# Transposes of a fused attention and GLU kernel: from the tensor engine to the DMA queues

## The chip, the cores and the metric

The kernel runs on one core of a Trainium2 chip. A core has a tensor engine (PE, with its weight loads shown as PEld), a vector engine (DVE), a scalar engine (ACT), GpSimd (POOL), and SyncE (SP), which here only issues DMAs. Matmul results land in PSUM; the other operands live in SBUF. The metric is the device time of one execution in microseconds (us). Before the change it was 374.96 us (median of 15 runs, 373.54 to 377.10). Each run carries a state, fast or slow; fast runs alone are compared here.

## The reference, cut to what matters

The input is 2048 tokens of width 640, in bfloat16. After a layernorm, the tokens go through a 32-head attention with a recurrent memory over four segments of 512 tokens, and through a gated unit. The two results are multiplied and added to the input.

```python
xn = layernorm(x)                               # no affine part
for s in range(4):                              # segments of 512 tokens
    a_dot = softmax(q @ k.T * scale + mask) @ v
    a_mem = phi(q) @ M / (phi(q) @ z + 1e-6)    # memory of earlier segments
    o     = g * a_mem + (1 - g) * a_dot
    M    += phi(k).T @ v;   z += sum(phi(k))    # phi(t) = t+1 if t>0 else exp(t)
s = o @ wo
h = sigmoid(xn @ w_gate) * (xn @ w_up);   y = h @ w_down
out = x + s * silu(y)
```

## The kernel before

The program is scheduled by hand. A segment has 24 slots, one for each of 8 head groups times 3 units of keys. A slot issues scores, one large Exp on ACT and the product with V. Between these, `fill` feeds dense matmuls (gate, up, down) to PE at an even pace, and a plan hangs smaller pieces on slots: the next segment's layernorm and projections, the memory read (`mem_part`, slots 0 to 7) and the memory update (slots 9 and 10). The plan fixes the order of each engine's instructions. Most matmul results share three PSUM buffers (`ps_d`, tag "d"), so PE waits when a buffer it wants has not been read out yet (two such waits are shown below).

Three tensors are needed in the other orientation. Each is transposed on PE, 128 tokens at a time, in a group of five 128x128 transposes into one PSUM buffer, followed by a copy:

```python
ps_d = ctx.enter_context(tc.tile_pool(name="ps_d", bufs=3, space=PSUM))

def ln_transpose(n, j, xn, eng):                 # normalized x
    pT = ps_d.tile([P, DC, P], BF, name="pT", tag="d")
    for c in range(DC):                          # DC = 5
        nc.tensor.transpose(pT[:, c, :], xn[:, c * P:(c + 1) * P], ident[:])
    ... nc.vector.tensor_copy(xnT_of[n][:, :, j * P:(j + 1) * P], pT[:])

def phiK_tok(n, j):                              # phi(K), to tokens on partitions
    pk = ps_d.tile([P, DC, P], BF, name="pk", tag="d")
    for c in range(DC):
        nc.tensor.transpose(pk[:, c, :], seg[n]["kt"][:, c, j * P:(j + 1) * P], ident[:])
    ... nc.vector.tensor_copy(t[:], pk[:].rearrange("p c t -> p (c t)"))

def out_T(n, j):                                 # attention output, before @ wo
    po = ps_d.tile([P, DC, P], BF, name="po", tag="d")
    for c in range(DC):
        nc.tensor.transpose(po[:, c, :], s["odot"][:, j, c * P:(c + 1) * P], ident[:])
    ... nc.scalar.mul(oT[:], po[:], 0.25)
```

K and Q also make a round trip through DRAM (`Kd`, `Qd`) to be laid out by head; this is there before and after.

## Time and profile before

| what | value | view |
|---|---|---|
| span of the profiled execution | 373.7 us | page |
| PE busy | 351.8 us, 94% | page, busy table |
| DVE and ACT busy | 231.9 us each, 62% | page, busy table |
| chain of work that ended last | 74% PE | page, chain |
| one group of five transposes | 0.29 us of PE | timeline |

The page of the kernel before, its span and busy table, the DMA totals, and the chain by engine (lines left out between them):

```profile
span 373.7 us, 8613 instructions
PE 351.8 (94%) x3569; PEld 196.9 (53%) x3569; DVE 231.9 (62%) x523; ACT 231.9 (62%) x246; POOL 103.4 (28%) x172
...
DMA packets 21527, 25.60 MB, mean 69 GB/s; under 512 B 1648, under 2 KB 20208, under 8 KB 21488
...
PE 74%; ACT 10%; DVE 8%; issue 3%; DMA 2%; POOL 1%; SPq 0%; POOLq 0%; ACTq 0%
```

PE is the engine to relieve. A busy PE is not PE at its peak, so the worth of a transpose is read from the timeline. This is the timeline of PE (start, length, line, operation, tiles, shapes, count):

```profile
45.90 0.41 PE L464 MATMUL Sps<-QT,KT 21*128 21x384 bf16 x8
46.24 0.45 PE L299 MATMUL pk<-ident,ktd 128*128 128x128 bf16 x5
46.53 1.24 PE L346 MATMUL gp<-xnT,Wg 128*128 128x512 bf16 x5
```

The group is printed as 0.45 us long, but the next group starts 0.29 us after it. That step is what a group costs. The copies out of PSUM are read from the groups of instructions (busy us, mean ns, then idle time before them):

```profile
L387 ACT ACTIVATE oT<-po 128x640 bf16<-128x640 bf16 x12 | 8.4, 700 | 1.2 <-PE po L385 0.9
...
L203 DVE COPY xnT<-pT 128x640 bf16<-128x640 bf16 x12 | 5.8, 484 | 1.1 <-PE pT L198 1.1
L301 DVE COPY phiktok<-pk 128x640 bf16<-128x640 bf16 x12 | 5.8, 482 | 0.0
```

PE is not full everywhere. In stretches of 10 us (us, then for each engine its busy time and count, then granted clock, DMA share, GB/s) it drops where a segment starts, while DVE is nearly full:

```profile
core 0: us, PE busy (x) PEld busy (x) DVE busy (x) ACT busy (x) POOL busy (x), PEclk, DMA share, GB/s
120.00:130.00 10.00, 8.45 (x100) 4.88 (x99) 9.62 (x28) 6.96 (x7) 2.37 (x4) 1.00 0.01 2
200.00:210.00 10.00, 8.50 (x94) 4.47 (x95) 9.69 (x26) 6.56 (x8) 3.27 (x4) 1.00 0.01 2
210.00:220.00 10.00, 8.39 (x90) 4.97 (x89) 8.29 (x25) 4.56 (x5) 3.32 (x6) 0.83 0.05 18
```

Among the waits of PE (us in total, times, longest) are two in which `gp` (a gate product) stands still for results that it does not use; what it waits for, by the code, is one of the three PSUM buffers:

```profile
PE gp L346 <- ACT oT L387: 1.0, 1, 1.0
...
PE gp L346 <- DVE aa L401: 0.9, 1, 0.9
```

### The profile page before, as it was taken

What the parts mean: (1) busy time and instruction counts of PE and PEld (TensorE: products, weight loads), DVE (VectorE), ACT (ScalarE), POOL (GpSimd) and SP (SyncE); (2) the same over time, 40 slices, a digit from 0 to 9 for tenths busy, and PEclk for the clock granted to TensorE, in tenths of its full rate; (3) what the DMA queues carried; (4) which work ended last, traced back from release to release, by engine and by line L of the source; (5) the groups of instructions that cost most, each with busy time, mean ns of one, the idle gap of its engine ahead of it and who ended that gap; (6) DMA issues with size and microseconds to landing.
All of it is one profiled execution on the core that took longest, in us unless ns stands there. A gap on an engine that the chain in (4) does not pass through costs nothing.

```text
span 373.7 us, 8613 instructions
## 1 busy us (share of the span) xinstructions
PE 351.8 (94%) x3569; PEld 196.9 (53%) x3569; DVE 231.9 (62%) x523; ACT 231.9 (62%) x246; POOL 103.4 (28%) x172
## 2 busy tenths in 40 slices
PE   6999999999999899999998799999989999999992
PEld 2643456555645466455565356555436755545661
DVE  5465966456549997756548977746744575533354
ACT  2436766656868765665777656555776677666730
POOL 7600232222232222222223222222212222221314
PEclk9999999999999999999999899999999999999997
DMA  7976820012521010012520001011402000100001
GB/s 237 381 260 197 251 88 3 0 44 69 136 67 46 3 35 19 19 44 92 153 68 6 0 19 37 19 44 47 125 3 71 3 2 19 38 18 3 2 2 70
DMA packets 21527, 25.60 MB, mean 69 GB/s; under 512 B 1648, under 2 KB 20208, under 8 KB 21488
## 3 DMA queue, kind: packets, MB, share of 16 engines
q1 hardware_dynamic: 20176, 21.12, 18.6%
q10 hardware_dynamic: 1312, 3.93, 2.7%
q8 instruction: 28, 0.46, 0.5%
q14 instruction: 11, 0.09, 0.1%
HBM read 17.05 MB, written 7.86 MB: 67 GB/s over the span
## 4 chain that ended last, share of the span: by engine, by line
PE 74%; ACT 10%; DVE 8%; issue 3%; DMA 2%; POOL 1%; SPq 0%; POOLq 0%; ACTq 0%
PE yp L369 13%; PE up L355 12%; PE gp L346 12%; PE psq L215 10%; PE Aps L488 7%; PE Sps L464 6%; ACT pt L472 6%; PE psv L273 5%; PE sp L399 4%; ACT mn L288 2%; DMA Wv<-in_A_wv_dram 2%; PE cps L259 1%; PE dm L312 1%; DVE omem L339 1%; DVE hT L358 1%
## 5 line engine op out<-in xcount | busy, mean ns | idle before, releaser
L472 ACT ACTIVATE pt<-Sps 128x2048 bf16<-128x2048 f32 (+1 forms) x96 | 152.9, 1593 | 41.3 <-PE Sps L464 39.9
L474 POOL TENSOR_SCALAR_AFFINE_SELECT pt<-pt 128x512 bf16<-128x512 bf16 x128 | 82.5, 655 | 254.7 <-ACT pt L472 254.7
L346 PE MATMUL gp<-xnT,Wg 128*128 128x512 bf16 x240 | 60.9, 385 | 3.2 <-DVE omem L339 1.1
L355 PE MATMUL up<-xnT,Wu 128*128 128x512 bf16 x240 | 59.7, 379 | 2.0 <-ACT tg L349 2.0
L369 PE MATMUL yp<-Wd,hT 128*128 128x320 bf16 x384 | 57.5, 299 | 0.0
L358 DVE SCALAR_TENSOR_TENSOR hT<-tg,up 128x512 bf16<-128x512 bf16 x48 | 32.6, 680 | 38.2 <-PE up L355 33.6
L488 PEld LDWEIGHTS <-pt 128*128 128x128 bf16 x1280 | 45.0, 96 | 20.1 <-issue 5.0
L488 PE MATMUL Aps<-V,pt 128*128 128x21 bf16 x1280 | 47.2, 173 | 2.6 <-DVE rm L336 1.0
L349 ACT ACTIVATE tg<-gp 128x512 bf16<-128x512 f32 x48 | 28.4, 596 | 24.7 <-PE gp L346 24.5
L369 PEld LDWEIGHTS <-hT 128*128 128x128 bf16 x384 | 35.2, 97 | 15.1 <-issue 2.2
L373 DVE SCALAR_TENSOR_TENSOR aa<-t,yp 128x320 bf16<-128x320 bf16 x32 | 15.5, 485 | 39.7 <-ACT t L372 39.7
L464 PE MATMUL Sps<-QT,KT 21*128 21x128 bf16 (+3 forms) x512 | 34.9, 302 | 0.6 <-ACT pt L472 0.4
L346 PEld LDWEIGHTS <-Wg 128*128 128x128 bf16 x240 | 21.0, 98 | 27.2 <-issue 6.5
L355 PEld LDWEIGHTS <-Wu 128*128 128x128 bf16 x240 | 21.2, 97 | 23.9 <-issue 3.9
L278 ACT CAST V<-psv 128x320 bf16<-128x320 f32 x32 | 13.7, 428 | 24.2 <-PE psv L273 24.0
L464 PEld LDWEIGHTS <-KT 21*128 21x128 bf16 x512 | 11.3, 91 | 30.8 <-issue 30.4
L273 PE MATMUL psv<-Wv,xnT 128*128 128x320 bf16 x160 | 26.1, 299 | 0.5 <-DMA Wv<-in_A_wv_dram 0.5
L372 ACT ACTIVATE t<-yp 128x320 bf16<-128x320 f32 x32 | 13.9, 436 | 19.5 <-PE yp L369 19.5
L215 PE MATMUL psq<-xnT,Wq 128*128 128x512 bf16 x100 | 24.3, 378 | 0.0
L215 PE MATMUL psq<-xnT,Wk 128*128 128x512 bf16 x100 | 24.3, 378 | 0.0
L220 DVE CAST ktd<-psq 128x512 bf16<-128x512 f32 x20 | 13.7, 687 | 15.8 <-PE psq L215 15.8
L399 PE MATMUL sp<-Wo,oT 128*128 128x320 bf16 x120 | 20.3, 300 | 1.0 <-DVE omem L339 1.0
(91 smaller groups left out, 363.7 us busy)
## 6 DMA issues: line engine op xcount, KB each, us to landing
KT<-Kd SPq DMA_DIRECT2D x32, 80.0 KB
QT<-Qd SPq DMA_DIRECT2D x32, 80.0 KB
out_dram<-xt SPq DMA_DIRECT2D x16, 160.0 KB
Wg<-in_B_w_gate_dram ACTq DMA_DIRECT2D x1, 1920.0 KB
Wu<-in_B_w_up_dram ACTq DMA_DIRECT2D x1, 1920.0 KB
xt<-in_A_x_dram SPq DMA_DIRECT2D x3, 640.0 KB
Wd<-in_B_w_down_dram SPq DMA_DIRECT2D x1, 1920.0 KB
Kd<-ktd SPq DMA_DIRECT2D x4, 384.0 KB
```

The source lines that it names most:

```text
L215: nc.tensor.matmul(ps[:], lhsT=W[:, k, c * P:(c + 1) * P], rhs=xnT_of[n][:, k, :], start=(k == 0), stop=(k == DC - 1))
L273: nc.tensor.matmul(ps[:], lhsT=xnT_of[n][:, k, j * P:(j + 1) * P], rhs=Wv[:, k, half * HD:(half + 1) * HD], start=(k == 0), stop=(k == DC ...
L346: nc.tensor.matmul(gp[:], lhsT=Wg[:, k, f * P:(f + 1) * P], rhs=xnT_of[n][:, k, :], start=(k == 0), stop=(k == DC - 1))
L349: nc.scalar.activation(tg[:], gp[:], ACT.Tanh, scale=0.5)
L355: nc.tensor.matmul(up[:], lhsT=Wu[:, k, f * P:(f + 1) * P], rhs=xnT_of[n][:, k, :], start=(k == 0), stop=(k == DC - 1))
L358: nc.vector.scalar_tensor_tensor(out=h[:], in0=seg[n]["tg"][:], scalar=1.0, in1=up[:], op0=ALU.add, op1=ALU.mult)
L369: nc.tensor.matmul(yp[:], lhsT=s["hT"][f][:, j * P:(j + 1) * P], rhs=Wd[:, f, hs], start=(f == 0), stop=(f == FC - 1))
L399: nc.tensor.matmul(sp[:], lhsT=s["po"][j][:, c, :], rhs=Wo[:, c, hs], start=(c == 0), stop=(c == DC - 1))
L464: nc.tensor.matmul(Sps[:, r, c0:c0 + ncol], lhsT=KT[32 * r:32 * r + E1, g, kb * P:(kb + 1) * P], rhs=QT[32 * r:32 * r + E1, g, q0:L], star ...
L472: nc.scalar.activation(pt[:, :, 0:ntot], Sps[:, :, 0:ntot], ACT.Exp, scale=SCALE)
L474: nc.gpsimd.affine_select(out=pt[:, :, c0:c0 + P], in_=pt[:, :, c0:c0 + P], compare_op=ALU.is_ge, fill=0.0, base=0, pattern=[[0, 4], [1, P ...
L488: nc.tensor.matmul(Aps[:, qb, r, :], lhsT=pt[:, r, off:off + P], rhs=V[n % 2][:, kb, 4 * g + r, :], start=(ui == 0 and r == 0 and qb == 0) ...
```

## The change

The intent is to take 180 of the transposes off PE. Each tensor is stored to DRAM in its natural layout (K is there already) and fetched with one 640 KB DMA transpose. The projection by `wo` starts four slots after the last store, to give the DMA time. phi(K) now acts on the transposed copy, and its Exp comes one slot after its minimum. In segment 0 it starts at slot 4, because its copy lands late. The factor 0.25 moves into the gates. SBUF room is found by letting `warm` share a buffer and by one `aa` buffer less. In segment 0, empty plan entries at slots 4 to 7 still count the time of four groups of transposes, so that `fill` puts less dense work there. Segment 0's layernorm and the last segment's output keep their PE transposes, because nothing could hide the latency there.

```diff
+    def ln_spill(n, j, xn):
+        nc.sync.dma_start(Xd[n % 2][j * P:(j + 1) * P, :], xn[:])
+
+    def ln_dmaT(n):
+        xnT_of[n] = xpool.tile([P, DC, L], BF, name="xnT")
+        nc.sync.dma_start_transpose(out=xnT_of[n][:], in_=Xd[n % 2][:])
...
-    def phiK_tok(n, j):
-        pk = ps_d.tile([P, DC, P], BF, name="pk", tag="d")
...
+    def k_tok(n):
+        seg[n]["ktok"] = stg.tile([P, 4, D], BF, name="ktok")
+        nc.sync.dma_start_transpose(out=seg[n]["ktok"][:], in_=Kd[n % 2][:])
...
-    def out_T(n, j):
-        po = ps_d.tile([P, DC, P], BF, name="po", tag="d")
...
+        nc.sync.dma_start(Od[n % 2][j * P:(j + 1) * P, :], s["odot"][:, j, :])
+
+    def out_T(n):
+        oT = fpool.tile([P, DC, L], BF, name="oT", bufs=1)
+        nc.sync.dma_start_transpose(out=oT[:], in_=Od[n % 2][:])
...
         for part in range(2):
-            at(2 * part, 0, phi, n, "kt", "phik", part)
-            at(2 * part + 1, 0, phi_end, n, "phik", part)
+            s0 = 4 if n == 0 else 0
+            at(s0 + 2 * part, 0, phi_min, n, "ktok", "phik", 2 * part, 2 * part + 2)
+            at(s0 + 2 * part + 1, 0, phi_exp, n, "phik", 2 * part)
+            at(s0 + 2 * part + 2, 0, phi_end, n, "phik", 2 * part)
         for j in range(4):
-            at(1 + j, 0, stats, j)
-            at(5 + j, 0, norm, j)
-            at(4 + j, TR_NS, phiK_tok, n, j)
-            at(6 + j, TR_NS, lambda j=j: ln_transpose(m, j, st[j], nc.vector))
+            at(j, 0, stats, j)
+            at(4 + j, 0, norm, j)
+        at(7, 0, ln_dmaT, m)
...
-        return deque([[A(0)], [A(1), T(0)], [M(0, 0)], [A(2), T(1), M(0, 1)], [M(1, 0)], [A(3), T(2), M(1, 1)],
-                      [M(2, 0)], [T(3), M(2, 1)], [M(3, 0)], [M(3, 1)]])
+        return deque([[A(0)], [A(1)], [A(2)], [A(3), T], [], [], []] + [[M(j, h)] for j in range(4) for h in range(2)])
```

More of the change, by code (lines that the diff above doesn't have):

```diff
@@ L89 @@
     Kd = [dpool.tile([D, L], BF, name=f"Kd{i}") for i in range(2)]
+    Xd = [dpool.tile([L, D], BF, name=f"Xd{i}") for i in range(2)]
+    Od = [dpool.tile([L, D], BF, name=f"Od{i}") for i in range(2)]
     ctx.enter_context(tc.manual_schedule(
@@ L115 @@
     Wu = cpool.tile([P, DC, F], BF, name="Wu")
-    warm = cpool.tile([P, L], BF, name="warm")
-    nc.vector.memset(warm[:], 0.0)
+    warm = stg.tile([P, 3 * L], BF, name="mn")
+    nc.vector.memset(warm[:, 0:L], 0.0)
     load_x(0, split=4)
@@ L167, in gates @@
         gcol = cpool.tile([P, H], F32, name="gcol")
-        nc.vector.tensor_scalar(gcol[:], th[:], 0.5, 0.5, op0=ALU.mult, op1=ALU.add)
-        nc.vector.tensor_scalar(omg[:], th[:], -0.5, 0.5, op0=ALU.mult, op1=ALU.add)
+        nc.vector.tensor_scalar(gcol[:], th[:], 0.125, 0.125, op0=ALU.mult, op1=ALU.add)
+        nc.vector.tensor_scalar(omg[:], th[:], -0.125, 0.125, op0=ALU.mult, op1=ALU.add)
         nc.vector.reciprocal(ginv[:], gcol[:])
@@ L280, in do_V, with phi, phi_min, phi_exp @@
             nc.vector.tensor_copy(dst, src)
-    def phi(n, key, name, part):
-        c0, c1 = ((0, 3), (3, 5))[part]
+    def phi(n, key, name, c0, c1):
         s = seg[n]
         src = s[key][:, c0:c1, :]
-        mn = stg.tile([P, 3, L], BF, name="mn")
-        nc.vector.tensor_scalar(mn[:, 0:c1 - c0, :], src, 0.0, None, op0=ALU.min)
-        nc.scalar.activation(mn[:, 0:c1 - c0, :], mn[:, 0:c1 - c0, :], ACT.Exp)
-        nc.vector.tensor_scalar(src, src, 0.0, None, op0=ALU.max)
-        s[name, part] = (src, mn[:, 0:c1 - c0, :])
-    def phi_end(n, name, part):
-        dst, ex = seg[n][name, part]
-        nc.vector.tensor_tensor(dst, dst, ex, op=ALU.add)
-    def phiK_tok(n, j):
-        pk = ps_d.tile([P, DC, P], BF, name="pk", tag="d")
-        for c in range(DC):
-            nc.tensor.transpose(pk[:, c, :], seg[n]["kt"][:, c, j * P:(j + 1) * P], ident[:])
-        t = stg.tile([P, D], BF, name="phiktok", bufs=4)
-        nc.vector.tensor_copy(t[:], pk[:].rearrange("p c t -> p (c t)"))
-        seg[n]["ktok", j] = t
+        mn = stg.tile([P, 3 * L], BF, name="mn")
+        w = src.shape[1] * src.shape[2]
+        m = mn[:, 0:w].rearrange("p (c n) -> p c n", n=src.shape[2])
+        nc.vector.tensor_scalar(m, src, 0.0, None, op0=ALU.min)
+        nc.scalar.activation(m, m, ACT.Exp)
+        nc.vector.tensor_scalar(src, src, 0.0, None, op0=ALU.max)
+        s[name, c0] = (src, m)
+    def phi_min(n, key, name, c0, c1):
+        s = seg[n]
+        src = s[key][:, c0:c1, :]
+        mn = stg.tile([P, 3 * L], BF, name="mn")
+        w = src.shape[1] * src.shape[2]
+        m = mn[:, 0:w].rearrange("p (c n) -> p c n", n=src.shape[2])
+        nc.vector.tensor_scalar(m, src, 0.0, None, op0=ALU.min)
+        nc.vector.tensor_scalar(src, src, 0.0, None, op0=ALU.max)
+        s[name, c0] = (src, m)
+    def phi_exp(n, name, c0):
+        m = seg[n][name, c0][1]
+        nc.scalar.activation(m, m, ACT.Exp)
+    def phi_end(n, name, c0):
+        dst, ex = seg[n][name, c0]
+        nc.vector.tensor_tensor(dst, dst, ex, op=ALU.add)
+    def k_tok(n):
+        seg[n]["ktok"] = stg.tile([P, 4, D], BF, name="ktok")
+        nc.sync.dma_start_transpose(out=seg[n]["ktok"][:], in_=Kd[n % 2][:])
     def m_update(n, part):
@@ L312, in m_update @@
                 nc.tensor.matmul(dm[:, MOFF[c] - o0:MOFF[c + 1] - o0],
-                                 lhsT=seg[n]["ktok", j][:, c * P:(c + 1) * P],
+                                 lhsT=seg[n]["ktok"][:, j, c * P:(c + 1) * P],
                                  rhs=V[n % 2][:, j, h0:h1 + 1, :].rearrange("p h e -> p (h e)"),
@@ L364, in do_down @@
         if half == 0:
-            s["aa"][j] = fpool.tile([P, D], BF, name="aa", bufs=5)
+            s["aa"][j] = fpool.tile([P, D], BF, name="aa", bufs=4)
         hs = slice(half * HD, (half + 1) * HD)
@@ L379, in out_add @@
             nc.vector.tensor_tensor(s["odot"][:, j, :], s["odot"][:, j, :], s["omem"][:, j, :], op=ALU.add)
-    def out_T(n, j):
-        s = seg[n]
-        po = ps_d.tile([P, DC, P], BF, name="po", tag="d")
-        for c in range(DC):
-            nc.tensor.transpose(po[:, c, :], s["odot"][:, j, c * P:(c + 1) * P], ident[:])
-        oT = fpool.tile([P, DC, P], BF, name="oT")
-        nc.scalar.mul(oT[:], po[:], 0.25)
-        s["po"][j] = oT
+        nc.sync.dma_start(Od[n % 2][j * P:(j + 1) * P, :], s["odot"][:, j, :])
+    def out_T(n):
+        oT = fpool.tile([P, DC, L], BF, name="oT", bufs=1)
+        nc.sync.dma_start_transpose(out=oT[:], in_=Od[n % 2][:])
+        seg[n]["oT"] = oT
     def out_store(n, j):
@@ L398, in out_mm @@
         for c in range(DC):
-            nc.tensor.matmul(sp[:], lhsT=s["po"][j][:, c, :], rhs=Wo[:, c, hs],
+            nc.tensor.matmul(sp[:], lhsT=s["oT"][:, c, j * P:(j + 1) * P], rhs=Wo[:, c, hs],
                              start=(c == 0), stop=(c == DC - 1))
@@ L422, in tail_T @@
         if j % 2:
-            nc.vector.tensor_scalar(oT, po[:], 0.25, None, op0=ALU.mult)
+            nc.vector.tensor_copy(oT, po[:])
         else:
-            nc.scalar.mul(oT, po[:], 0.25)
+            nc.scalar.copy(oT, po[:])
     def tail_acc(i):
@@ L443, in tail_end @@
             nc.tensor.transpose(po[:, j, :], s["odot"][:, j, C4:D], ident[:])
-        oT = fpool.tile([P, DC, P], BF, name="oT")
-        nc.scalar.mul(oT[:, 0:4, :], po[:], 0.25)
+        oT = fpool.tile([P, DC, L], BF, name="oT", bufs=1)[:, 0, :].rearrange("p (j t) -> p j t", t=P)
+        nc.scalar.copy(oT, po[:])
         for i in range(8):
@@ L507, in keep_warm @@
         for _ in range(k):
-            nc.tensor.matmul(wps[:], lhsT=warm[:, 0:P], rhs=warm[:], start=True, stop=True)
+            nc.tensor.matmul(wps[:], lhsT=warm[:, 0:P], rhs=warm[:, 0:L], start=True, stop=True)
     keep_warm(11)
@@ L560 @@
     gates()
+    k_tok(0)
     nc.sync.dma_start(Wd[:], B_w_down.rearrange("(f p) n -> p f n", p=P))
@@ L591, in norm @@
         def norm(j):
-            st[j] = ln_norm(m, j, st["mv"], st["rs"])
+            ln_spill(m, j, ln_norm(m, j, st["mv"], st["rs"]))
         for part in range(2):
-            at(2 * part, 0, phi, n, "kt", "phik", part)
-            at(2 * part + 1, 0, phi_end, n, "phik", part)
+            s0 = 4 if n == 0 else 0
+            at(s0 + 2 * part, 0, phi_min, n, "ktok", "phik", 2 * part, 2 * part + 2)
+            at(s0 + 2 * part + 1, 0, phi_exp, n, "phik", 2 * part)
+            at(s0 + 2 * part + 2, 0, phi_end, n, "phik", 2 * part)
         for j in range(4):
-            at(1 + j, 0, stats, j)
-            at(5 + j, 0, norm, j)
-            at(4 + j, TR_NS, phiK_tok, n, j)
-            at(6 + j, TR_NS, lambda j=j: ln_transpose(m, j, st[j], nc.vector))
+            at(j, 0, stats, j)
+            at(4 + j, 0, norm, j)
+        at(7, 0, ln_dmaT, m)
+        for j in range(4 if n == 0 else 0):
+            at(4 + j, TR_NS, lambda: None)
         at(9, 800, m_update, n, 0)
@@ L617, in segment_plan @@
         at(18, 0, bound_dma, m, 0, [nc.sync])
-        at(18, 0, phi, m, "qt", "phiq", 0)
+        at(18, 0, phi, m, "qt", "phiq", 0, 3)
         at(19, 0, phi_end, m, "phiq", 0)
@@ L622, in segment_plan @@
         at(21, C_NS, bound_mm, m, 1, None)
-        at(21, 0, phi, m, "qt", "phiq", 1)
-        at(22, 0, phi_end, m, "phiq", 1)
+        at(21, 0, phi, m, "qt", "phiq", 3, 5)
+        at(22, 0, phi_end, m, "phiq", 3)
+        if m < NSEG - 1:
+            at(21, 0, k_tok, m)
         if n + 2 < NSEG:
@@ L630, in out_steps @@
         A = lambda j: (0, lambda: out_add(n, j))
-        T = lambda j: (TR_NS, lambda: out_T(n, j))
+        T = (0, lambda: out_T(n))
         M = lambda j, h: (V_NS, lambda: out_mm(n, j, h))
-        return deque([[A(0)], [A(1), T(0)], [M(0, 0)], [A(2), T(1), M(0, 1)], [M(1, 0)], [A(3), T(2), M(1, 1)],
-                      [M(2, 0)], [T(3), M(2, 1)], [M(3, 0)], [M(3, 1)]])
+        return deque([[A(0)], [A(1)], [A(2)], [A(3), T], [], [], []] + [[M(j, h)] for j in range(4) for h in range(2)])
     dense = deque()
```

## The prediction

> **What bounds the kernel.** The profile's busy table gives PE 351.8 of 373.7 us (94%), DVE and ACT 62% each; the chain of work that ended last is 74% PE. The stretches of 10 us show PE at 10.00 nearly everywhere; it falls to 8.4-9.1 only at the start (0-10), the tail (360-370), and where a new segment begins (120-140, 200-230), where DVE is at 8.1-9.7. There the waits list 2.6 us (118-145) and 4.7 us (200-232) of PE waiting, mostly for DVE (omem, aa, hT, rm) or ACT's oT. The clock drops to 0.83 in 210-220.
>
> **What the change removes.** For segments 1-3 the layernorm transposes (pT), for 0-2 those of phi(K) (pk) and of the attention output (po): 36 groups of five, 180 matmuls. In the timeline each group advances PE by 0.29 us (46.24 to 46.53): 36 x 0.29 = 10.4 us. Also DVE 24 x 0.48 = 11.6 us, ACT's oT 12 x 0.70 = 8.4 us, and 36 turns of the PSUM buffers.
>
> **What it adds.** 24 stores (12 xn, 12 odot tiles) of 160 KB and nine 640 KB DMA transposes on SP's queue. phi(K) acts on the transposed copy, same elements, its Exp one slot later. The 0.25 moves into the gates, free.
>
> **Is the DMA latency hidden?** Queues are nearly idle after 50 us (mean 69 GB/s). The plain 640 KB x load at 112-115 us takes about 3 us, near 250 GB/s. The Trainium skill, "DMA: Bandwidth & Descriptors", section "Latency and other measured facts", gives about 261 GB/s for DMA transposes; its page "VectorE: DVE Perf Modes", section "The three transpose paths", gives 1309 ns for one 128x128 block, which, if blocks did not overlap, would be 20 x 1.3 = 26 us for ours. No trace here shows which. My estimate: 4-8 us from issue to landing, plus about 2.5 us for the store. A slot is about 3.45 us (83 us / 24). xnT has about 3.5 slots (12 us) from the last norm to its first use, oT about 4 slots (14 us), ktok 3 slots before phi(K) and far more before its matmuls. SP issues in order, so a late odot store delays xn stores and xnT behind it; I expect under 1 us of PE wait per segment from it.
>
> **Sum.** 376.6 - 10.4 (PE) - 2.5 (less waiting at segment starts, as DVE loses 3.9 us per segment and ACT 2.8) + 1.3 (new exposure to xnT/oT) = **365.0 us**, range 359 to 374. Faster by over 2% (under 369.1): 0.75; within 2%: 0.17; slower by over 2%: 0.08.
>
> **What would show each step.** Right: PE has 180 matmuls less and its busy time falls by about 10 us; ACT about 8, DVE about 12 less; no PE wait over 1 us released by the xnT or oT transposes; PE nearer 10 in 120-140 and 200-230.
>
> **What would make it wrong.** (1) Transposes slow (over 10 us): PE would wait on the xnT DMA before the first K projection of segments 1-3, on oT before sp, and DVE on ktok; at 26 us that costs some 15 us per segment and the change is slower. (2) The transpose holding up SP's queue, so that KT/QT relayouts or Wd land late. (3) Segment starts bound by ACT's Exp or by DVE work that stays (mem_part, hT): then PE work saved there is returned as waiting and the gain shrinks to 5-7 us, within 2%.

## More of the kernel before

The granted clock was 0.50 from 212.1 to 215.5 us, from the second of two short gaps of PE on (in brackets: idle time before, and what ended it):

```profile
210.95 0.44 PE L299 MATMUL pk<-ident,ktd 128*128 128x128 bf16 x5 [0.75 <-DVE hT L358]
212.25 2.29 PE L346 MATMUL gp<-xnT,Wg 128*128 128x512 bf16 x5 [0.86 <-DVE aa L401]
```

A group of `gp` usually takes 1.24 us. From group start to group start in that stretch (2.09 us for `gp`, where 1.08 is usual, and less for the three groups after it), I estimate that the half clock cost this execution 1.4 us. Not every execution has it: of the 25 fast runs of this kernel in the calls of the experiments, seven have a mean clock of 0.990 or less and average 376.2 us, and the other 18, at 0.993 or more, average 374.3.

## The result, and the profile after

The changed kernel took 361.05 us (median of 12 runs, 359.69 to 366.03; the last was a slow run), against 374.96 us before. The ratio is 0.9628, with a 95% interval of 0.9601 to 0.9656: faster, by about 13.9 us. Ratios here are the mean time of one kernel's fast runs over that of the other's of the same rounds, so they are not quite the ratio of the medians.

The page of the changed kernel, same parts as above:

```profile
span 358.4 us, 8274 instructions
PE 341.6 (95%) x3389; PEld 185.9 (52%) x3389; DVE 221.0 (62%) x499; ACT 223.8 (62%) x234; POOL 104.5 (29%) x172
...
DMA packets 48309, 35.40 MB, mean 99 GB/s; under 512 B 25360, under 2 KB 46992, under 8 KB 48272
...
PE 75%; ACT 9%; DVE 9%; POOL 2%; issue 2%; DMA 2%; SPq 0%; POOLq 0%; ACTq 0%
```

PE has 180 matmuls and 10.2 us of busy time less, DVE 10.9 us and ACT 8.1 us less. PE's idle time, span less busy, went from 21.9 to 16.8 us. PE is still the bound. Part of this is luck: the execution profiled before lost about 1.4 us to the half clock, mostly as PE busy time, and this one has no half clock before its tail. The 23,712 added packets under 512 B are nearly all the nine transposes: 640 KB in packets of 256 B is 2560 packets each.

The stretches where segments start (the second segment's first Exp is now at 109 us, the third's at 189; before, at 112 and 195):

```profile
110.00:120.00 10.00, 9.35 (x95) 4.34 (x93) 9.59 (x26) 7.16 (x8) 3.07 (x4) 1.00 0.24 69
120.00:130.00 10.00, 9.46 (x96) 4.43 (x95) 8.90 (x24) 6.83 (x8) 4.37 (x6) 1.00 0.10 35
190.00:200.00 10.00, 9.36 (x102) 5.25 (x101) 9.59 (x27) 7.39 (x9) 2.72 (x4) 1.00 0.06 20
200.00:210.00 10.00, 8.77 (x87) 4.05 (x85) 9.65 (x27) 6.25 (x6) 4.16 (x6) 1.00 0.19 67
```

DVE is as full there as before, but PE loses less. The first xnT transpose on SP's timeline:

```profile
56.42 2.75 SPq L212 DMA_TRANSPOSE xnT<-Xd  x1
```

The DMA traffic after it, in half microseconds (the last two columns are the busy share of the DMA engines and GB/s):

```profile
57.00:57.50 0.50, 0.50 (x5) 0.20 (x3) 0.50 (x1) 0.50 (x2) 0.00 (x0) 1.00 0.00 0
57.50:58.00 0.50, 0.50 (x18) 0.50 (x17) 0.39 (x2) 0.50 (x1) 0.00 (x0) 1.00 0.35 79
...
60.00:60.50 0.50, 0.50 (x7) 0.12 (x6) 0.17 (x1) 0.00 (x0) 0.00 (x0) 1.00 1.28 291
60.50:61.00 0.50, 0.50 (x8) 0.38 (x5) 0.50 (x1) 0.32 (x1) 0.00 (x0) 1.00 0.41 86
61.00:61.50 0.50, 0.50 (x6) 0.35 (x4) 0.01 (x1) 0.50 (x1) 0.00 (x0) 1.00 0.00 0
```

The first matmuls that read xnT, on PE's timeline:

```profile
64.86 1.24 PE L224 MATMUL psq<-xnT,Wk 128*128 128x512 bf16 x5
```

The transpose is issued at 56.4 us, its packets run from about 57.7 to 60.7, and the data is wanted at 64.9. No PE wait in the whole profile is released by an xnT or an oT transpose by DMA (the `oT` in this complete list, L462, is an ACT copy in the tail):

```profile
PE Aps L505 <- POOL pt L491: 1.7, 6, 0.4
PE up L375 <- ACT tg L369: 1.5, 5, 0.6
PE wps L525 <- DVE mn L120: 1.2, 1, 1.2
PE sp L452 <- DVE aa L472: 1.2, 1, 1.2
PE Aps L505 <- DVE odot L517: 0.9, 2, 0.7
PE Sps L481 <- ACT pt L489: 0.8, 2, 0.4
PE Aps L505 <- DVE rm L356: 0.8, 2, 0.5
PE Sps L467 <- ACT oT L462: 0.7, 1, 0.7
PE pT L200 <- DVE xn L186: 0.5, 2, 0.3
PE psv L282 <- DMA Wv<-in_A_wv_dram: 0.5, 1, 0.5
PE gp L366 <- DVE hT L378: 0.2, 1, 0.2
PE po L435 <- DVE aa L393: 0.2, 1, 0.2
```

The latency is hidden, and the two waits of `gp` shown before are gone.

### The profile page after: what moved, and what is told of

Its sections match the earlier page's. It is cut to its first block, busy times and chain, and to the rows that moved or that the text cites. A ratio compares the mean times of both kernels' runs of the same rounds, so it can differ in the third digit from the quotient of the medians.

```text
span 358.4 us, 8274 instructions
## 1 busy us (share of the span) xinstructions
PE 341.6 (95%) x3389; PEld 185.9 (52%) x3389; DVE 221.0 (62%) x499; ACT 223.8 (62%) x234; POOL 104.5 (29%) x172
## 4 chain that ended last, share of the span: by engine, by line
PE 75%; ACT 9%; DVE 9%; POOL 2%; issue 2%; DMA 2%; SPq 0%; POOLq 0%; ACTq 0%
PE yp L389 13%; PE gp L366 13%; PE up L375 12%; PE psq L224 10%; PE Aps L505 8%; PE Sps L481 6%; ACT pt L489 6%; PE psv L282 5%; PE sp L416 4%; DMA Wv<-in_A_wv_dram 2%; DVE st L177 2%; PE cps L268 1%; POOL pt L491 1%; DVE hT L378 1%; DVE omem L359 1%
## 5 line engine op out<-in xcount | busy, mean ns | idle before, releaser
L491 POOL TENSOR_SCALAR_AFFINE_SELECT pt<-pt 128x512 bf16<-128x512 bf16 x128 | 83.5, 663 | 237.7 <-ACT pt L489 237.7
L366 PE MATMUL gp<-xnT,Wg 128*128 128x512 bf16 x240 | 59.7, 379 | 0.3 <-DVE hT L378 0.2
L505 PEld LDWEIGHTS <-pt 128*128 128x128 bf16 x1280 | 44.1, 96 | 23.2 <-issue 5.6
L392 ACT ACTIVATE t<-yp 128x320 bf16<-128x320 f32 x32 | 14.0, 437 | 16.8 <-PE yp L389 16.8
L282 PEld LDWEIGHTS <-xnT 128*128 128x128 bf16 x160 | 15.5, 98 | 10.7 <-ACT xnT L203 1.0
```

The costliest lines, as they stand in the source:

```text
L282: nc.tensor.matmul(ps[:], lhsT=xnT_of[n][:, k, j * P:(j + 1) * P], rhs=Wv[:, k, half * HD:(half + 1) * HD], start=(k == 0), stop=(k == DC ...
L366: nc.tensor.matmul(gp[:], lhsT=Wg[:, k, f * P:(f + 1) * P], rhs=xnT_of[n][:, k, :], start=(k == 0), stop=(k == DC - 1))
L491: nc.gpsimd.affine_select(out=pt[:, :, c0:c0 + P], in_=pt[:, :, c0:c0 + P], compare_op=ALU.is_ge, fill=0.0, base=0, pattern=[[0, 4], [1, P ...
L505: nc.tensor.matmul(Aps[:, qb, r, :], lhsT=pt[:, r, off:off + P], rhs=V[n % 2][:, kb, 4 * g + r, :], start=(ui == 0 and r == 0 and qb == 0) ...
```

## The experiments

There were twelve runs, all of them correct. My theory, A, was that PE is the limit, so the 10.4 us of transposes are the gain, and that some more comes from less waiting. Rival B was that PE has room, and the relief of DVE, ACT and the PSUM buffers is the gain. Rival C was that the new schedule (phi(K), statistics) is what lowers the waiting. Where a difference "over the changed kernel" is given in us, it is the difference of the two ratios to before, times 375 us. Kernels are compared only within the same rounds.

### Putting the removed work back

`pe_back` adds the 36 groups as dead work to the changed kernel:

```diff
+    def dead(eng):
+        pd = ps_d.tile([P, DC, P], BF, name="pdead", tag="d")
+        for c in range(DC):
+            nc.tensor.transpose(pd[:, c, :], Wq[:, 0, c * P:(c + 1) * P], ident[:])
...
+        for j in range(4):
+            at(4 + j, TR_NS, dead, nc.vector)
+            at(6 + j, TR_NS, dead, nc.vector)
```

Four more per segment go into the output steps.

> The changed kernel plus the 36 groups of five PE transposes at the old places, on a constant operand, their PSUM result read by nobody. Theory A (the tensor engine is the limit, its 10.4 us of transposes are the gain): loses 10 to 11 us against the changed kernel, about 371 to 372 us, ratio to before about 0.99. Rival B (the gain is the relief of DVE, ACT and the PSUM buffers, PE has room): stays within 2 us of 361.

It took 372.68 us (median of 4), ratio 0.9905 (0.9829 to 0.9981): 10.4 us over the changed kernel (0.9905 - 0.9628, times 375; with both intervals, about 7.4 to 13.4). That agrees with the predicted PE time, though the exact match is luck. In the profile PE's busy time is back at 351.8 us, 10.2 more than in the changed kernel, without a half clock before the tail. B, which allowed 2 us, falls as far as DVE and ACT are concerned; the dead groups also take turns of the PSUM buffers, so this run does not separate those from PE time.

`cp_back` puts back only the DVE and ACT time, with no PE work and no PSUM buffer:

```diff
+    def dead(eng):
+        t = stg.tile([P, 3, L], BF, name="aq")[:].rearrange("p c n -> p (c n)")[:, 0:D]
+        if eng is nc.scalar:
+            nc.scalar.copy(t, Wq[:, 0, :])
+        else:
+            nc.vector.tensor_tensor(t, Wq[:, 0, :], Wq[:, 1, :], op=ALU.add)
```

> The changed kernel plus 24 DVE operations (128x640, about 0.5 us) and 12 ACT copies (128x640, about 0.7 us) at the old places, no PE transposes. Theory A: DVE is full only at segment starts, so this gives back the 2 to 4 us of PE waiting that vanished there: about 363 to 365 us. Rival B: gives back nearly all, about 371 to 375. Rival C (the smaller waiting comes from the moved schedule of phi(K) and statistics, not from fewer copies): within 1 us of 361.

It took 362.18 us (median of 4), ratio 0.9669 (0.9598 to 0.9739): 1.5 us over the changed kernel, though DVE is back at 230.9 us and ACT at 231.6 us busy. This is less than A expected, but the interval, from below zero to 4 us, separates neither A's 2 to 4 us nor C's 1 us. B's 10 to 14 us are excluded: relieving DVE and ACT is worth little by itself.

`both_back` has the dead transposes and, tied to them, the copies out of their PSUM buffers:

```diff
+        (the transposes of pe_back, then)
+        if eng is nc.scalar:
+            nc.scalar.copy(t, pd[:].rearrange("p c t -> p (c t)"))
+        else:
+            nc.vector.tensor_copy(t, pd[:].rearrange("p c t -> p (c t)"))
```

> The changed kernel plus dead PE transposes and their evacuations, 24 on DVE and 12 on ACT, at the old places; all DMA transposes stay. Theory A: back to the time of before, 373 to 376 us (ratio 0.995 to 1.005), so the DMA path itself costs nothing and the new schedule gains nothing. Rival C (schedule): stays 3 to 5 us under before. If the DMA path costs time, it is above before.

It took 376.65 us (median of 4, the profiled one, 392.14 us, slow), ratio 1.0023 (0.9950 to 1.0097). With the old work back, the old time is back, though all nine DMA transposes and the new schedule are still in place. So the DMA path and the new schedule together change nothing beyond the interval (2 us less to 4 us more than before). A small cost of one and a small gain of the other could cancel. Also, the dead transposes read a constant and never wait for their data, as the real ones could. C's 3 to 5 us are excluded, so it falls as the main cause.

`untied` is `both_back` with DVE and ACT reading SBUF constants instead of the PSUM buffers:

```diff
-            nc.vector.tensor_copy(t, pd[:].rearrange("p c t -> p (c t)"))
+            nc.vector.tensor_tensor(t, Wq[:, 0, :], Wq[:, 1, :], op=ALU.add)
```

> As both_back (dead PE transposes, 24 DVE and 12 ACT operations of the same length at the same places), but the DVE and ACT operations read a constant in SBUF, not the PSUM buffer that PE has just filled. pe_back cost 11.6 us and cp_back 1.1 us over the changed kernel, both_back 15. If the excess of both_back comes from PE waiting for the evacuation of a shared PSUM buffer: additive here, about 373 to 374. If it comes from the DVE and ACT time as such beside the PE time: as both_back, 375.5 to 377.

It took 374.47 us (median of 6), ratio 0.9985 (0.9951 to 1.0020). Over the changed kernel, PE work alone costs 10.4 us and copies alone 1.5, which sums to 11.9; untied costs 13.4 and tied 14.8. The order is what the shared PSUM buffer would give, but the intervals of these two overlap almost wholly. The 1.5 to 3 us beyond the sum are within the intervals. Whether they are real, and come from the buffer or from engine time, stays open.

### One third of the change at a time

Each of these is the kernel before with the hunks of one part or two. The only plan edits are those of that part. None of them has the empty entries in segment 0, which stand in the changed kernel alone.

```diff
 only_xn:  +ln_spill, +ln_dmaT; stats at j, norm at 4+j, ln_dmaT at 7; -ln_transpose at 6+j
 only_o :  +Od store, out_T by DMA, output steps with three empty slots; 0.25 into the gates
 only_k :  +k_tok, phi_min/phi_exp/phi_end on ktok; -phiK_tok
 xn_k   :  only_xn and only_k together
```

> The kernel before with only the layernorm transposes of segments 1 to 3 moved to DMA: 12 of the 36 groups. Theory A: 12 x 0.29 = 3.5 us of PE time plus up to 1.5 us less waiting: gain 3.5 to 5 us, about 370 to 371. If the parts do not add up (the gain hangs on all three together, or on one of them): under 2 us, or over 8 us.

> The kernel before with only the transposes of the attention output moved to DMA, which also moves the output projection 3 to 4 slots later: 12 of the 36 groups. Theory A: 3.5 us of PE time plus up to 1.5 us less waiting (the profile before charges 1.5 us of PE waiting to the ACT copies of these): gain 3.5 to 5 us, about 370 to 371.

> The kernel before with only phi(K) on a DMA-transposed copy, with its new schedule: 12 of the 36 groups. Theory A: 3.5 us of PE time plus up to 1.5 us less waiting: gain 3.5 to 5 us, about 370 to 371; with the two other parts the gains add to 12 to 15 us. Rival C (the schedule of phi(K) is the main gain): over 6 us here and under 3 us in the two others.

> The kernel before with two parts of the change, xnT and phi(K) by DMA, and the attention output still transposed on PE. Alone they gained about 3.1 and 4.7 us, the third 0.7 to 1.0, the whole change 13.9. If these two are additive: 7 to 9 us, near 367, and then the third part, nearly worthless alone, is worth 5 to 6 us once the others are gone. If these two already reinforce each other: 10 us or more, near 364, and the third adds its 3.5 us of PE time.

| kernel | median us | ratio to before | 95% interval | gain, us (1 - ratio, times 375) |
|---|---|---|---|---|
| only_xn | 371.52 | 0.9919 | 0.9888 to 0.9951 | 3.0 |
| only_o | 373.86 | 0.9973 | 0.9938 to 1.0008 | 1.0 |
| only_k | 370.04 | 0.9868 | 0.9830 to 0.9906 | 5.0 |
| xn_k | 364.91 | 0.9745 | 0.9713 to 0.9777 | 9.6 |
| all three (control) | 360.12 | 0.9615 | 0.9584 to 0.9646 | 14.4 |

The parts do not add up: alone they give 9.0 us, together about 14. The third part is worth 1.0 us alone (interval about 0 to 2.3) but, with the empty entries of segment 0, 4.9 us (0.9745 - 0.9615, times 375; about 3.2 to 6.6) once the other two are in. I had expected 3.5 to 5 us of it alone, so that expectation missed. Of `only_xn` I had also expected 3.5 to 5 us; it gave 3.0 (1.8 to 4.2). `xn_k` gave 9.6, between the two readings of its expectation.

The 4.9 us cannot be put down to the third part alone. Segment 0 transposes no attention output, yet in the profiles it lasts 79.9 us in `xn_k` and 76.5 us in the changed kernel (first Exp to next segment's first Exp), with ten gate and up matmuls fewer in it. Those matmuls run later, and no run has the third part without the empty entries that move them, so their share stays open.

The stretches of `only_o` where the third segment starts show PE waiting there:

```profile
200.00:210.00 10.00, 7.47 (x86) 4.40 (x80) 9.41 (x26) 7.48 (x8) 3.01 (x4) 1.00 0.06 20
210.00:220.00 10.00, 8.03 (x92) 4.30 (x92) 8.93 (x24) 5.15 (x6) 4.24 (x6) 1.00 0.14 49
```

Before, PE had 8.50 and 8.39 us there; now it has 7.47 and 8.03, with DVE again near full. (Some 1% of the matmul records are missing from this trace, so PE's figures are a little low, and this segment starts 2.6 us later than before.) The waits of PE from 195 to 235 us in the same run:

```profile
PE gp L347 <- DVE hT L359: 1.8, 1, 1.8
PE gp L347 <- ACT tg L350: 1.6, 1, 1.6
PE Sps L462 <- ACT pt L470: 0.9, 1, 0.9
PE gp L347 <- DVE omem L340: 0.3, 1, 0.3
```

Between 205 and 214 us the chain of work that ended last runs through DVE nearly step after step: phi(K), statistics, `odot`, `hT`, `omem`. My reading is that this part takes PE work out of a stretch where DVE is the limit (it moves the projection to later slots as well), so PE gives time back as waiting. The list does not prove it: it sums to 4.6 us, and the same stretch before has 4.7 us of waits, besides the half clock. Also, this execution reached its first Exp 1.7 us later than the one before (34.4 against 32.7), with 2.1 against 0.5 us of PE waits on the weights Wv and Wq; why is not known. The two other parts take 24 copies off DVE, eight in each of the first three segments. That this is why the third gains more with them is not shown either; no run isolates it from the PSUM turns, which go with the copies, or from the empty entries of segment 0.

### How much latency is hidden

`late2` moves the norms and the transpose two slots later; the transpose has to follow the norms, because SP issues it when its data is there, whatever slot the line stands in (in the chain below at 63.16 us, when the store had landed at 63.00).

```diff
-            at(4 + j, 0, norm, j)
-        at(7, 0, ln_dmaT, m)
+            at(6 + j, 0, norm, j)
+        at(9, 0, ln_dmaT, m)
```

> The changed kernel with the norms and the xnT transpose two slots (6.8 us) later, everything else in place. In the trace of the changed kernel xnT lands 3.0 to 3.9 us before its first use in each of three segments. If that margin is real and PE stands still meanwhile: PE waits about 3 to 4 us on xnT in each of segments 1 to 3, about 10 us in all, 371 us. If other work fills in or the margin is larger than read: under 3 us lost.

It took 371.34 us (median of 4), ratio 0.9911 (0.9848 to 0.9974): 10.6 us over the changed kernel, as expected. The waits of PE (us in total, times, longest):

```profile
PE psq L224 <- DMA xnT<-Xd: 8.5, 3, 4.6
...
```

Part of the chain from 60 to 72 us in the same run (start, us, what):

```profile
61.23 1.77 DMA Xd<-xn
...
63.16 6.19 DMA xnT<-Xd
...
```

The timeline of PE there:

```profile
69.39 2.29 PE L224 MATMUL psq<-xnT,Wk 128*128 128x512 bf16 x5 [4.56 <-DMA xnT<-Xd]
```

The issue on SP and the release of PE in the next segment:

```profile
148.73 2.67 SPq L212 DMA_TRANSPOSE xnT<-Xd  x1
...
153.57 1.25 PE L224 MATMUL psq<-xnT,Wk 128*128 128x512 bf16 x5 [1.93 <-DMA xnT<-Xd]
```

The clock in the first of these gaps (the third column from the right):

```profile
67.50:68.00 0.50, 0.00 (x0) 0.00 (x0) 0.00 (x0) 0.00 (x0) 0.00 (x0) 0.50 0.01 1
```

PE waited three times, 8.5 us in all. A store landed 1.8 us after its issue and the first transpose 6.2 us after it. In the next two segments it was 4.8 us, 0.5 us after the last packet of the transpose. In the first, a few packets came late: the others had ended near 67.3 us, the last at 68.7. The end of the packets that I had read as the landing comes earlier than the release. In the changed kernel the packets of all three xnT transposes end 4.3 us after the issue. With 0.5 us more, which is an estimate, the margins before the first use are 3.6, 2.6 and 2.5 us, where I had written 3.0 to 3.9: all under one slot.

The matmul group after the 4.56 us gap also took 2.29 us where 1.24 is usual. The granted clock was 0.50 from 67.2 to 74.0 us. The Trainium skill, "TensorE: Matmul & The Clock Gate", part 1, says that the clock is at half after at least one idle window of about 3.4 us. The half clock agrees with this case; the idle time does not. Here the clock fell 2.4 us after PE's last matmul, in the kernel before it fell at 212.1 us in the second of two gaps of only 0.75 and 0.86 us, and the gap of 1.93 us above left it at 1.00. So the first missed DMA was paid twice: the slower `psq` and `yp` groups (2.29 against 1.24 us, 2.80 against 1.80) add about 2 us to the 8.5, together about the 10.6 us that were lost.

### Looking for something better

`spread` spreads the memory read over 12 slots, to relieve DVE where a segment starts.

```diff
-                at(i, MEM_NS, mem_part, n, i // 2, i % 2)
+                at((0, 2, 3, 5, 6, 8, 9, 11)[i], MEM_NS, mem_part, n, i // 2, i % 2)
-        at(9, 800, m_update, n, 0)
-        at(10, 520, m_update, n, 1)
+        at(12, 800, m_update, n, 0)
+        at(13, 520, m_update, n, 1)
```

> The changed kernel with the eight memory-read pieces of a segment (three DVE operations each) spread over slots 0 to 11 instead of 0 to 7, and the memory update moved from slots 9 and 10 to 12 and 13. In the changed kernel DVE is busy 9.6 of 10 us where segments 1 and 2 start, and PE idles about 3 us in all there. If DVE is what PE waits for there: 1.5 to 3 us faster than the changed kernel, about 358.5 to 359.5. If it is ACT or the mask on GpSimd: within 1 us of it.

It took 362.71 us (median of 4), ratio 0.9677 (0.9647 to 0.9707). It is no faster than the changed kernel; by the ratios it is 1.8 us slower, but the intervals overlap. PE's waits for the mask on POOL went from 1.7 to 3.5 us and those for `odot` on DVE from 0.9 to 2.4. The waiting moved. Why it grew was not tested.

`k_later_q` starts phi(K) at slot 4 in all segments, and also separates the Exp of phi(Q) from its minimum by a slot. `after_again` is the changed kernel as a control.

```diff
-            s0 = 4 if n == 0 else 0
+            s0 = 4
-        at(18, 0, phi, m, "qt", "phiq", 0, 3)
-        at(19, 0, phi_end, m, "phiq", 0)
+        at(18, 0, phi_min, m, "qt", "phiq", 0, 3)
+        at(19, 0, phi_exp, m, "phiq", 0)
+        at(20, 0, phi_end, m, "phiq", 0)
... (and the second half of phi(Q) in the same way, at slots 21 to 23)
```

> The changed kernel with phi(K) of segments 1 and 2 begun at slot 4 instead of 0 (as segment 0 has it), so that DVE has 4 us less in the first four slots of a segment, and with the Exp of phi(Q) one slot after its minimum. In the changed kernel PE idles some 3 us at the two segment starts, where DVE is at 9.6 of 10, and 2 to 3 us around slots 18 to 21. If both are cured: 358 to 359.5 us. If as with the spread of the memory reads the waits only move: 361 to 363.

> The changed kernel itself, as a control on the same chip and in the same rounds: 361 us, ratio to before 0.960 to 0.966.

`k_later_q` took 358.10 us (median of 6, 357.15 to 359.90), ratio 0.9567 (0.9534 to 0.9599). The control took 360.12 us (median of 6, one of them slow at 365.66; its five fast runs 359.87 to 360.90), ratio 0.9615 (0.9584 to 0.9646). The means of the fast runs, 358.39 and 360.19, differ by 1.8 us, and only the slowest of its six runs reaches into the control's range. It is the fastest of all versions run. The intervals of the two ratios still overlap a little, and the two edits were not run apart, so which one helps is open.

## Why the prediction was right

- **Time.** 365.0 us was predicted and 361.05 measured, inside the range of 359 to 374, and faster by over 2% as forecast. The gain was taken from 376.6 us as 11.6; it was 13.9. The 376.6 us were the median of the first three runs of the kernel before; over all 15 it is 374.96.
- **What is removed.** Right, and shown. 180 matmuls went; PE's busy time fell by 10.2 us (10.4 predicted; some 1.4 of the 10.2 are the half clock before), DVE's by 10.9 (about 12), ACT's by 8.1 (about 8). Putting the transposes back alone cost 10.4 us and 10.2 us of PE's busy time, the latter without a half clock.
- **Latency hidden.** Right, and shown. The guess of 4 to 8 us from issue to landing holds: 4.8, 4.8 and 6.2 us where the landing can be read. A store took 1.8 us, where I had about 2.5. The reading of 26 us is excluded. Risk (2), a transpose that holds up KT, QT or Wd on SP's queue, did not show: none of these stands in the list of PE's waits.
- **New exposure of 1.3 us.** This term was too large. No PE wait in the changed kernel is released by a DMA of xnT or oT, and with the old work back the time is that of before, within its interval.
- **Less waiting, 2.5 us, "as DVE loses 3.9 us per segment and ACT 2.8".** The size was too small and its reason only half right. 13.9 to 14.4 us, less 10.4 of PE time, leaves about 4 us. But DVE and ACT time alone, put back, costs 1.5 us (with an interval that reaches from nothing to 4). A part that I overlooked is the half clock: no fast run of the changed kernel here has a mean clock below 0.994. Seven of 25 runs before at 1.9 us each would be about 0.5 us (an estimate). The rest, if it is more than noise, showed only when PE's transposes and the copies stood together, and what couples them was not settled.
- **PE nearer 10 at the segment starts.** Only partly. At 120-130 and 200-210 PE had 8.45 and 8.50; the four stretches after have 8.77 to 9.46. DVE is as full as before there.
- **Risk (3), segment starts bound by DVE work that stays.** It did not decide the result. DVE is at 9.4 of 10 us at a segment start of `only_o`, which gained 1.0 us where its PE time is 3.5, so a third of this change alone would have been called no gain. That DVE ate the difference is likely, not shown.

## What to carry to other kernels

When PE is the bound and the DMA queues are idle, a PE transpose with its PSUM turn can be traded for a DMA transpose, provided its first use lies some three slots, here 10 us, behind the last producer: in `late2`, store and transpose together took 6.6 to 8 us, and PE paid for what lay beyond the margin, in one of three cases with a lowered clock as well. Cost such a removal by the step in the timeline, not by the printed length. Before judging one part of a change alone, ask which engine limits the stretch that it relieves, and compare it only in kernels that are otherwise the same: here a part that gained 1.0 us alone seemed to gain 4.9 with the others, but one more plan edit came in with it.

## What the Trainium skill lacked or had wrong

- "VectorE: DVE Perf Modes", section "The three transpose paths", gives 390 ns for a 128x128 transpose on TensorE and 1309 ns by DMA. Neither serves as a cost in a stream: here five transposes advanced PE by 0.29 us, 58 ns each, and 20 blocks in one DMA landed 4.8 to 6.2 us after issue, 0.24 to 0.31 us each.
- "DMA: Bandwidth & Descriptors", section "Latency and other measured facts", gives a bandwidth for DMA transposes but no time from issue to landing. Here the instruction held SP's queue for 2.6 to 4.8 us, the first packets came about 1.3 us after issue, and 640 KB landed after 4.8 us twice and 6.2 us once.
- The same section names 261 GB/s for a non-contiguous case and 350 to 400 GB/s for a contiguous one. Here, with a contiguous DRAM source, half-microsecond slices of a transpose alone reached about 290 GB/s in packets of 256 B, between the two. Over all its packets (640 KB in 3.0 us) the mean is about 218 GB/s, below both. Which of the two cases this transpose is remains unclear. The prediction named 261 GB/s without its condition.
- "TensorE: Matmul & The Clock Gate" gives no length for idle times shorter than its window that lower the clock. Here gaps of 0.75 and 0.86 us, with 0.44 us of work between them, came before 3.4 us at a clock of 0.50, and a gap of 1.93 us did not lower it.
